# Two key tiles' scores in one run over three PSUM slots, and a planner with other durations and ranks

## The chip, the cores and the metric

The kernel runs on one core of one Trainium2 chip. The metric is the device time of one execution in microseconds. PE is TensorE, DVE is VectorE, ACT is ScalarE, POOL is GpSimd, SP is SyncE; L414 is line 414 of the kernel.

## The reference

A thresholded attention is followed by a feed-forward block with a quick GELU. All numbers are float32.

```python
# q, k, v: (8, 8, 576, 64)   tau = 0.02
scores = scale * np.matmul(q, k.transpose(0, 1, 3, 2))
thresh = np.max(scores, axis=-1, keepdims=True) - tau
scores = np.where(scores >= thresh, scores, -1000000000.0)
scores = scores - np.max(scores, axis=-1, keepdims=True)
attn = np.exp(scores)
attn = attn / (np.sum(attn, axis=-1, keepdims=True) + 1e-09)
attn_out = np.matmul(attn, v)
x = attn_out.transpose(0, 2, 1, 3).reshape(4608, 512)
h = x @ w_in                                  # w_in  (512, 2048)
g = h * (1.0 / (1.0 + np.exp(-1.702 * h)))
out = g @ w_out                               # w_out (2048, 512)
```

The two weights come as 64-bit floats and are turned into 32-bit ones on the chip.

## The kernel before

**Attention.** The 64 heads are 32 pairs (`n`), four pairs a batch. A pair's two heads lie on partitions 0 to 63 and 64 to 127. The scores are held transposed, keys on partitions: four tiles of 128 keys with both heads side by side (128 x 1152), and a tail tile with the last 64 keys of both heads (128 x 576). For a pair, in turn:

- `load_qk`, `load_v` (SP's DMA queue), `prep` (L390, DVE transposes q and k), `prep_kd` (L395, POOL copies the tail keys of both heads into a block-diagonal `kd`).
- `scores` (L414, two matmuls at a time on half of PE's rows; the tail, L407, with `kd` on the full array) into PSUM slots of the pool `psA`, which has three slots of two banks. Each slot is copied to SBUF by `keep` (L437, ACT) and then is free.
- `in_groups` (L451, DVE: transpose and reduce over groups of 32 keys), `over_tiles` (L457, L462), `over_groups` (the folds, L471, L472) give the maximum; `lower` and `spread_max`, or for the first pairs `lower_rows`, `row_out` and `row_in` (a round trip by DMA), spread the threshold; `sub` (L523 to L528, DVE), `mask` (L534, ACT), `exps` (L538, ACT).
- `values` (L552, half of PE's columns, 40 records a pair) into a `psA` slot that stays taken until `place_x`; sums of the weights by PE (`sums_by_pe`) for pairs 0 to 4, by DVE afterwards (`one_group`, L595); `spread_sums` (L604, L606); `place_x` (L623, DVE) scales the values, writes them into `xT` and frees the slot.

**Feed-forward.** 18 blocks of 256 tokens. The first two run plainly: `mm1_0` (L678) for 16 column tiles `j`, `tanh` (ACT) and `gelu_0` (DVE), then `mm2` (L660). The next twelve run `mm1` (L638), `tanh`, `gelu` (L650), and `second` (L825): a product in seven half-size products P1 to P7 in place of eight, for which POOL makes sums of weight quarters once (`t_sum`, L785) and sums of activations for each block (`s_sums`, L791 to L793; `s_last`, L804). The last four blocks run in two pairs by `two_blocks`, where the first product is made in the same way (`product1`, L743) from sums made by `w_sum` (L717, DVE and POOL) and `x_sum` (L726, DVE), which need all of the attention's buffers to be free. `read` (L840, L847) takes the products out of PSUM.

**Order.** The kernel orders its work itself. Each piece is a task with an engine, a cost in us, a rank, the tasks it comes after, and the pools it takes from and gives to. `run_in_order` plays the tasks through on the host: whenever an engine is free it starts the ready task of lowest rank whose pools have room. The order in which tasks start is the order of the instructions in each engine's queue; on the chip an instruction waits only for the data and buffers it needs, and for its queue.

```python
def task(engine, cost, rank, f, *a, after=(), take=(), give=(), lag=0.06):
    if 0 <= rank < LAST:
        rank += CV.get(f.__name__, 0.0) + (EARLY if a[0] < 2 * NPAIR else LATER).get(f.__name__, 0.0)
...
for rank, i in sorted(queue):
    take = tasks[i][6]
    if all(free[pool] >= take.count(pool) for pool in set(take)):
        break
```

`EARLY` and `LATER` are the ranks' corrections for pairs 0 to 7 and the rest. The conversion of a weight piece is `cv_ex` (L353), `cv_frac` (L367, L371) and `cv_end` (L379) on DVE and `cv_power` on ACT; 32 pieces of 128 x 512 come by POOL's DMA queue.

Of the kernel before, what the change touches and what calls it, by code (L numbers as in the profile page):

```python
# [10 lines left out]
FP32 = mybir.dt.float32  # L11
# [19 lines left out]
def kernel(  # L31
# [97 lines left out]
    for x in ("raw0", "raw1", "qkT0", "qkT1", "mb"):  # L129
# [6 lines left out]
        "lower_rows": -1.89,  # L136
        "values": 1.63,
        "exps": 1.38,
        "load_qk": -1.72,
        "prep": -1.69,  # L140
        "load_v": 1.46,
        "mask": 1.64,
        "over_groups": -1.9,
        "sub": -1.05,
        "one_group": 0.95,
        "scores": 0.67,
        "spread_sums": 1.4,
        "sums_by_pe": 2.29,
        "in_groups": 0.61,
        "keep": -1.15,  # L150
    }
    LATER = {
        "in_groups": 0.38,
        "mask": -0.74,
    }
    CV = {
        "cv_power": 0.15,
        "cv_frac": 0.13,
    }

    def task(engine, cost, rank, f, *a, after=(), take=(), give=(), lag=0.06):
        if 0 <= rank < LAST:
            rank += CV.get(f.__name__, 0.0) + (EARLY if a[0] < 2 * NPAIR else LATER).get(f.__name__, 0.0)
        tasks.append((engine, cost, rank, f, a, [x for x in after if x is not None],
                      take, give, lag))
        return len(tasks) - 1
# [3 lines left out]
    def run_in_order():  # L170
# [10 lines left out]
        started = 0  # L181
        while events:
# [18 lines left out]
            for engine, queue in ready.items():  # L201
# [12 lines left out]
                heapq.heappush(events, (now + tasks[i][1], 0, i))  # L214
# [187 lines left out]
    def scores(n, t, c):  # L402
        qT, kT = mats[n, 0], mats[n, 1]
        ps = psA.tile([P, 2, 512], FP32, name="ps", tag="ps")
        if t == NKT:
            for i in range(2):
                nc.tensor.matmul(  # L407
                    ps[:, i, 0:SH], lhsT=kd, rhs=qT[:, ts(i, SH)],
                    start=True, stop=True,
                )  # L410
            del mats[n, 0], mats[n, 1]
        else:
            for h in range(2):
                nc.tensor.matmul(  # L414
                    ps[:, h, 0:SH],
                    lhsT=kT[ts(h, D), ts(t, P)], rhs=qT[ts(h, D), ts(c, SH)],
                    start=True, stop=True,
                )
        pss[n, t, c] = ps

    def scores_of(n, t, cs):
        for c in cs:
            scores(n, t, c)
# [474 lines left out]
    FFU = 1.722  # L898
# [3 lines left out]
    for i in range(len(pieces)):  # L902
# [9 lines left out]
        a = task("POOL", 2.4, rank, load_w, i, after=w_loads[-1:], take=place, lag=5.0)  # L912
        w_loads.append(a)
        e = task("DVE", 0.43, rank, cv_ex, i, after=[a])
        m = task("ACT", 0.79, rank, cv_power, i, after=[e])
        a = task("DVE", 1.14, rank, cv_frac, i, after=[e])

        over = [ready_w[y] for y in range(i) if i >= n_in and stage(y) == (i - n_in) // PER_STAGE]
        ready_w.append(task("DVE", 0.7, rank, cv_end, i, after=[a, m] + over, give=place))
# [8 lines left out]
    def first_blocks():  # L928
        xs = list(placed.values())[-NPAIR:]
        for j in range(NFC):  # L930
# [7 lines left out]
            a = task("ACT", 0.6, FIRST, tanh, j, after=ffn[-1:], take=("io",))  # L938
            gelus[j] = task("DVE", 0.69, FIRST, gelu_0, j, after=[a], give=("psM", "io"))
        for i in range(PLAIN * BLK // P):  # L940
# [7 lines left out]
            a = task("ACT", 0.6, FIRST, half, i, after=ffn[-1:], take=("osb",), give=("psM",))  # L948
            task("SP", 0.6, FIRST, store_0, i, after=[a], give=("osb",), lag=2.2)

        for x in range(4):
            for k in range(2):
                after = t_ready[-1:] + (ffn[-1:] if x > 1 else ffn[2 * NFC : 2 * NFC + 1])
                t_ready.append(
                    task("POOL", 3.0, FIRST, t_sum, x, k, after=after + ready_w[n_in:])
                )

    def feed_forward(blk):
# [3 lines left out]
        for j in range(HF):  # L962
            for f in range(2):
# [6 lines left out]
            a = task("ACT", 0.6, FIRST, tanh, j, after=ffn[-1:], take=("io",))  # L970
            gelus[j] = task(
                "DVE", 0.69, FIRST, gelu, j, after=[a, last_mm2.get(j // 4)],
                give=("psM", "io"),
            )
            if j % 2:
                sums.append(task("POOL", 2.5, FIRST, s_sums, j // 2, after=[gelus[j - 1], gelus[j]]))
        second(blk, 0, {j: [gelus[j]] for j in range(HF)}, sums)

    def second(blk, w, ready, sums):
# [4 lines left out]
        for x, p in order:  # L984
            js = ((0, 4), (4, 8), (4, 7), (7, 8))[p]
            after = ffn[-1:] + t_ready
# [15 lines left out]
            if x == P6:  # L1002
                lasts = [task("POOL", 1.6, FIRST, s_last, k, w, after=ffn[-1:]) for k in range(2)]
            if x == P1:
                a = task("ACT", 0.35, FIRST, read, blk, x, after=ffn[-1:], take=("osb", "osb"))
            else:
                a = task(
                    "DVE", 0.84 if x == P5 else 0.42, FIRST, read, blk, x, after=ffn[-1:] + reads,
# [8 lines left out]
    def two_blocks(blk):  # L1017
# [4 lines left out]
        for x in range(4):  # L1022
            if first:
                done_w.append([task("DVE", 0.66, LAST - 1.0, w_sum, x, 0, nc.vector, after=done_w[-1:][0] if done_w else xs)])
            after = (xd[-1:] or xs) + (done_w[x][:1] if first else []) + last_product1
            xd.append(task("DVE", 0.66, LAST - 1.0, x_sum, blk, x, after=after))
        if first:
            for k in range(1, HF // 2):
                for x in range(4):
                    after = xs + done_w[x - 1][-1:] + done_w[x][-1:]  # L1030
                    done_w[x].append(
                        task("POOL", 1.5, FIRST, w_sum, x, k, nc.gpsimd, after=after)
# [3 lines left out]
        for j in range(HF):  # L1036
            reads = [None] * 7
            for x in range(7):
# [6 lines left out]
                if x == P3:  # L1045
                    after += xs
# [5 lines left out]
                if x == P1:  # L1052
                    a = task("ACT", 0.35, FIRST, read1, j, x, after=ffn[-1:], take=("hs",), give=bank)
                else:
                    a = task(
                        "DVE", 0.84 if x == P5 else 0.42, FIRST, read1, j, x,
# [3 lines left out]
            for h in range(2):  # L1060
                a = task("ACT", 0.6, FIRST, tanh1, j, h, after=[reads[P5 if h == 0 else P3]], take=("io",))
                g1[j, h] = task(
                    "DVE", 0.8, FIRST, gelu1, j, h, after=[a, last_mm2.get(j // 4), g1.get((j, 0))],
                    give=("io", "hs") if h else ("io",),
                )
            if j % 2:
                sums.append(task(
                    "POOL", 2.5, FIRST, s_sums, j // 2, after=[g1[j - 1, 0], g1[j, 0]]
# [5 lines left out]
        a = task("DVE", 1.3, FIRST, s_sum1, 0, after=again + ffn[-3:-2])  # L1074
        b = task("DVE", 1.3, FIRST, s_sum1, 1, after=[a] + ffn[-1:])
        c = task("DVE", 1.3, FIRST, s_sum1, 2, after=[b])
# [7 lines left out]
    for n in range(NP):  # L1084
# [4 lines left out]
        slow = 1.2 if n < NPAIR else 1.0  # L1089
# [11 lines left out]
        pq = task("DVE", 0.77, r, prep, n, 0, after=[lq], take=own(n, "qkT0"), give=own(n, "raw0"))  # L1101
        pk = task("DVE", 0.77, r, prep, n, 1, after=[lk], take=own(n, "qkT1"), give=own(n, "raw1"))
        pd = task("POOL", 0.5, r, prep_kd, n, after=[pk], take=("kd",))
# [5 lines left out]
        mx = []  # L1109
        for t in range(NKT + 1):  # L1110
            tail = t == NKT
            copies = []
            if tail or n >= WHOLE:


                cs = range(1 if tail else 2)
                a = task(
                    "PE", (1.2 if tail else 1.35) * slow, r, scores_of, n, t, cs, after=[pq, pk] + ([pd] if tail else []) + after,
                    take=("psA", "s_t") if tail else ("psA", "psA") + own(n, "s_m"),
                    give=own(n, "qkT0", "qkT1") + ("kd",) if tail else (),  # L1120
                )
                after = [a]
                copies = [task("ACT", 0.65, r, keep, n, t, c, after=[a], give=("psA",)) for c in cs]
            else:
                for c in range(2):

                    a = task(
                        "PE", 0.6 * slow, r, scores, n, t, c, after=[pq, pk] + after,
# [3 lines left out]
                    copies.append(task("ACT", 0.65, r, keep, n, t, c, after=[a], give=("psA",)))  # L1132
            mx.append(task("DVE", 0.76 if tail else 1.37, r, in_groups, n, t, ALU.max, after=copies))
# [100 lines left out]
```

## Time and profile before

| | us |
|---|---|
| timed runs | 1387.58, 1389.71, 1392.3 |
| profiled execution, span | 1385.8 |
| PE busy | 1330.6 |
| DVE busy | 1123.9 |
| ACT busy | 639.6 |
| POOL busy | 299.8 |

Busy times say how much an engine did, not whether it set the end; that is read stage by stage, from the waits and from the chain of work that ended last. A matmul's end is modelled in the profile, so differences between starts are used below. The profiler shows two records for each float32 matmul.

### The profile page before, as it was taken

Reading aid. Unit: us, or ns where it says so; the run is one execution under the profiler, and the core shown is the slowest. Engines: PE = TensorE matmul, PEld = TensorE weight load, DVE = VectorE, ACT = ScalarE, POOL = GpSimd, SP = SyncE. Lnnn points to the kernel's source line nnn. Section 1 sums busy time; section 2 is a strip of 40 time slices with the busy share of each in tenths; the row PEclk is TensorE's granted clock in tenths of the full one; section 3 lists DMA queues with packets and bytes.
Section 4 is the critical chain, followed back from the end, with each engine's and each line's share of the span. In section 5 each row is a group of like instructions: output and inputs, shape, how many; then the busy total and the mean of one; then the engine's idle time right before and its main releaser. Section 6 shows DMA issues by size and latency. Waiting matters only on the chain.

```text
span 1385.8 us, 18139 instructions
## 1 busy us (share of the span) xinstructions
PE 1330.6 (96%) x6792; PEld 1004.2 (72%) x6792; DVE 1123.9 (81%) x1906; ACT 639.6 (46%) x822; POOL 299.8 (22%) x362
## 2 busy tenths in 40 slices
PE   5778999999999999999999999999999999799999
PEld 3446864477777777777777777777777777688887
DVE  7989999978888888889888888888888888762642
ACT  5864663555454545454545445444545454120210
POOL 1121222212131213122212212121212224321120
PEclk9889999999999999999999999999999999999999
DMA  8674973211111111111111011111111100000000
GB/s 173 200 235 132 301 256 67 68 22 22 41 27 41 27 41 21 39 26 34 26 33 35 18 42 26 42 26 42 26 34 25 42 1 8 9 1 16 16 1 31
DMA packets 205379, 78.70 MB, mean 57 GB/s; under 512 B 192747, under 2 KB 192747, under 8 KB 205291
## 3 DMA queue, kind: packets, MB, share of 16 engines
q1 hardware_dynamic: 195723, 43.71, 15.0%
q0 software_dynamic: 7200, 33.55, 7.0%
q8 instruction: 53, 0.87, 0.2%
q10 hardware_dynamic: 2368, 0.30, 0.2%
q14 instruction: 35, 0.29, 0.1%
HBM read 68.05 MB, written 9.47 MB: 56 GB/s over the span
## 4 chain that ended last, share of the span: by engine, by line
PE 84%; DVE 12%; DMA 1%; issue 1%; SPq 1%; ACT 0%; DVEq 0%
PE hps L638 25%; PE ops L825 24%; PE ps L414 9%; PE pv L552 9%; PE ps L743 4%; PE hps L678 4%; PE ps L825 3%; PE ops L743 3%; DVE part L451 3%; PE ps L407 2%; DVE arena L523 2%; SPq L278 1%; PE den L552 1%; DVE red L472 1%; DVE arena L390 1%
## 5 line engine op out<-in xcount | busy, mean ns | idle before, releaser
L451 DVE TRANSPOSE_TENSOR_REDUCE part<-arena 128x36 f32<-128x1152 f32 x236 | 315.3, 1354 | 71.6 <-ACT arena L437 70.9
L638 PE MATMUL hps<-xT,w_in 128*128 128x256 f32 x1536 | 346.3, 382 | 0.0
L638 PEld LDWEIGHTS hps<-xT,w_in 128*128 128x128 f32 x1536 | 287.9, 190 | 56.3 <-issue 18.5
L437 ACT COPY arena<-ps 128x576 f32<-128x576 f32 x288 | 171.1, 641 | 292.3 <-PE ps L414 271.2
L825 PE MATMUL ops<-w_out,arena 128*128 128x256 f32 x896 | 205.5, 382 | 0.0
L534 ACT ACTIVATE arena<-arena 128x1152 f32<-128x1152 f32 (+1 forms) x160 | 168.2, 1060 | 76.3 <-DVE arena L523 70.2
L538 ACT ACTIVATE arena<-arena,shift,scl 128x1152 f32<-128x1152 f32 (+1 forms) x160 | 194.4, 1243 | 1.9
L825 PEld LDWEIGHTS ops<-w_out,arena 128*128 128x128 f32 x896 | 168.0, 190 | 32.8 <-issue 10.0
L523 DVE TENSOR_TENSOR arena<-arena 128x1152 f32<-128x1152 f32 x128 | 190.6, 1528 | 1.3 <-DMA arena<-row 0.6
L414 PE MATMUL ps<-arena 64*128 64x288 f32 x1024 | 162.0, 439 | 21.9 <-DVE arena L390 11.0
L791 POOL TENSOR_TENSOR arena<-arena 128x256 f32<-128x256 f32 x56 | 46.5, 831 | 566.5 <-DVE arena L650 467.4
L414 PEld LDWEIGHTS ps<-arena 64*128 64x128 f32 x1024 | 90.7, 191 | 84.7 <-issue 52.0
L825 PE MATMUL ops<-arena 128*128 128x256 f32 x672 | 149.9, 379 | 0.3 <-DVE osb L847 0.3
L825 PEld LDWEIGHTS ops<-arena 128*128 128x128 f32 x672 | 127.6, 190 | 18.0 <-DVE osb L847 0.7
L552 PE MATMUL pv<-arena 128*64 128x288 f32 x960 | 126.0, 414 | 1.2 <-issue 1.2
L647 ACT ACTIVATE th<-hps 128x512 f32<-128x512 f32 x112 | 66.4, 593 | 127.0 <-PE hps L638 106.0
L552 PEld LDWEIGHTS pv<-arena 128*64 128x64 f32 x960 | 67.0, 138 | 55.7 <-issue 14.6
L390 DVE STREAM_TRANSPOSE arena<-arena 128x576 f32<-128x576 f32 x64 | 48.3, 762 | 37.7 <-PE ps L407 35.3
L804 POOL TENSOR_TENSOR arena<-arena 128x512 f32<-128x512 f32 x28 | 57.5, 2060 | 98.6 <-PE ops L825 98.5
L650 DVE SCALAR_TENSOR_TENSOR arena<-th,hps 128x512 f32<-128x512 f32 x96 | 63.8, 665 | 8.8 <-ACT th L647 8.8
L395 POOL COPY kd<-arena 64x64 f32<-64x64 f32 x64 | 17.6, 275 | 235.0 <-DVE arena L390 191.2
L847 DVE SCALAR_TENSOR_TENSOR osb<-ops,osb 128x256 f32<-128x256 f32 x98 | 38.6, 405 | 34.9 <-PE ops L825 33.2
(122 smaller groups left out, 1422.4 us busy)
## 6 DMA issues: line engine op xcount, KB each, us to landing
arena<-in_q_dram SPq DMA_DIRECT2D x128, 72.0 KB, 2.2
out_dram<-osb SPq DMA_DIRECT2D x36, 256.0 KB, 2.0
arena<-in_k_dram SPq DMA_DIRECT2D x124, 72.0 KB, 2.2
arena<-in_v_dram SPq DMA_DIRECT2D x64, 128.0 KB, 2.4
w_out<-in_moe_w_in_dram POOLq DMA_DIRECT2D x12, 512.0 KB, 5.8
arena<-in_moe_w_out_dram POOLq DMA_DIRECT2D x12, 512.0 KB, 5.4
w_out<-in_moe_w_in_dram POOLq DMA_DIRECT2D x12, 511.6 KB, 7.0
arena<-in_moe_w_out_dram POOLq DMA_DIRECT2D x12, 511.6 KB, 6.3
```

Source lines behind the costliest of these rows:

```text
L414: nc.tensor.matmul(ps[:, h, 0:SH], lhsT=kT[ts(h, D), ts(t, P)], rhs=qT[ts(h, D), ts(c, SH)], start=True, stop=True,)
L437: nc.scalar.copy(out=o, in_=pss.pop((n, t, c))[:, :, 0:SH])
L451: nc.vector.tensor_reduce(out=o, in_=i, axis=AXL.X, op=op, apply_transpose=True)
L523: nc.vector.tensor_tensor(out=s, in0=s, in1=mb, op=ALU.subtract)
L534: nc.scalar.activation(out=s, in_=s, func=AF.Prelu, alpha=STEEP)
L538: nc.scalar.activation(out=s, in_=s, func=AF.Exp, scale=scl, bias=shift)
L552: nc.tensor.matmul(o[c][ts(h, D), 0:SH], lhsT=lhsT, rhs=rhs, start=(t == 0), stop=(t == NKT),)
L638: nc.tensor.matmul(hidden[j][:, ts(f, BLK)], lhsT=w_in[:, c, ds((f * HF + j) * P, P)], rhs=xTs[blk][:, c, :], start=(c == 0), stop=(c == N ...
L647: nc.scalar.activation(out=ths[j], in_=hidden[j], func=AF.Tanh, scale=GELU_SCALE / 2)
L650: nc.vector.scalar_tensor_tensor(out=g[:, :, j, :], in0=two(ths.pop(j)), scalar=1.0, in1=two(hidden.pop(j)), op0=ALU.add, op1=ALU.mult,)
L743: nc.tensor.matmul(places[j, x], lhsT=left[:, c, ts(j, P)], rhs=right[:, c, :], start=(c == 0), stop=(c == 1),)
L825: nc.tensor.matmul(banks[blk][k][:, ts(o, HM)], lhsT=left[:, j, :], rhs=right[:, j, :], start=(j == 0), stop=(j == HF - 1),)
```

## The change

Pairs from the seventh on (`WHOLE = 6`) make their scores by `scores_two`: two key tiles in one run of eight matmuls, in three `psA` slots taken together. The first 320 queries of each tile have a slot of their own, the last 256 queries of both tiles share the third. `keep_two` copies them, four copies for two tiles as before (128 x 640 and 128 x 512 in place of 128 x 576). The eight `t_sum` tasks come after the first product of block 2 instead of after the first blocks' first product, and only the products that read them come after them in the plan. The first `two_blocks` comes after all pairs in the plan. `tau_terms` comes after the first `prep`. The planner has new costs, a delay between engines (`LAG`), a cost for a change of PE's layout (`ENTER`), and new ranks for nearly every task.

```diff
     EARLY = {
-        "lower_rows": -1.89,
-        "values": 1.63,
...
+        "exps": 18.84,
+        "in_groups": 6.03,
...
+    LAG = {"PE": 0.26, "DVE": 0.18, "ACT": 0.22, "POOL": 0.18}
...
+    ENTER = (0.2, 0.1, 0.1)
...
+                if engine == "PE":
+                    last, mode = mode, MODES[tasks[i][3].__name__]
+                    cost += ENTER[mode] if mode != last else 0.0
...
+    FAR = S - BLK
+
+    def scores_two(n, t):
+        near = [psA.tile([P, 2, 512], FP32, name="ps", tag="ps") for _ in range(2)]
+        far = psA.tile([P, 2, 512], FP32, name="ps", tag="ps")
+        for u, part in ((0, 0), (0, 1), (1, 1), (1, 0)):
+            qs = ds(FAR, BLK) if part else ds(0, FAR)
+            for h in range(2):
+                o = far[:, h, ts(u, BLK)] if part else near[u][:, h, 0:FAR]
                 nc.tensor.matmul(
-                    ps[:, i, 0:SH], lhsT=kd, rhs=qT[:, ts(i, SH)],
+                    o, lhsT=mats[n, 1][ts(h, D), ts(t + u, P)], rhs=mats[n, 0][ts(h, D), qs],
                     start=True, stop=True,
                 )
...
+    def keep_two(n, t, c):
+        if c == 0:
+            sT[n, t] = seat_scores(n, t).rearrange("p (h s) -> p h s", h=2)
+        o = sT[n, t][:, :, ds(FAR, BLK)] if c else sT[n, t][:, :, 0:FAR]
+        nc.scalar.copy(out=o, in_=pss.pop((n, t, c)))
...
-        for x in range(4):
-            for k in range(2):
-                after = t_ready[-1:] + (ffn[-1:] if x > 1 else ffn[2 * NFC : 2 * NFC + 1])
-                t_ready.append(
-                    task("POOL", 3.0, FIRST, t_sum, x, k, after=after + ready_w[n_in:])
-                )
...
+            if j == T_AFTER and blk == PLAIN:
+                for y in range(8):
+                    after = t_ready[-1:] + ffn[-1:] + ready_w[n_in:]
+                    t_ready.append(task("POOL", 2.4, FIRST, t_sum, *divmod(y, 2), after=after))
...
-            after = ffn[-1:] + t_ready
+            after = ffn[-1:]
+            if x in T_OF:
+                after += t_ready[: T_OF[x]]
...
-                if x == P3:
+                if x == P3 or first:
                     after += xs
...
+        if n == 0:
+            tasks[tau_done][5].extend([pq, pk])
...
+            if n >= WHOLE and not tail:
+                if t % 2 == 0:
+                    a = task(
+                        "PE", 1.94, r, scores_two, n, t, after=[pq, pk] + after,
+                        take=("psA",) * 3 + ("s_m",) * 2,
+                    )
+                    after = [a]
+                b = task("ACT", 0.6, r, keep_two, n, t, 0, after=[a], give=("psA",))
+                c = task(
+                    "ACT", 0.48, r, keep_two, n, t, 1, after=[a, b] + far, give=("psA",) * (t % 2)
+                )
+                far = [c] if t % 2 == 0 else []
+                copies = [b, c]
...
-            mx.append(task("DVE", 0.76 if tail else 1.37, r, in_groups, n, t, ALU.max, after=copies))
+            mx.append(task("DVE", 0.66 if tail else 1.27, r, in_groups, n, t, ALU.max, after=copies))
```

## The prediction

> **What bounds the kernel now.** I read the page's busy table and slices first, then the windows by stage, the waits of TensorE, and the timeline where those waits lie.
>
> ```profile
> PE 1330.6 (96%) x6792; PEld 1004.2 (72%) x6792; DVE 1123.9 (81%) x1906; ACT 639.6 (46%) x822; POOL 299.8 (22%) x362
> ...
> PE   5778999999999999999999999999999999799999
> DVE  7989999978888888889888888888888888762642
> ```
>
> PE is full from about slice 5 on; only the start (DVE as full) and one slice near the end are not. So three stages: a start set by DVE, a long even stretch set by PE, and a passage to the last four blocks. The windows confirm it: PE is busy 150.00 of 150.00 us in each window from 350 to 1100, DVE 128. Who PE waits for:
>
> ```profile
> PE den L552 <- ACT arena L538: 16.8, 5, 5.6
> ...
> PE ps L414 <- DVE xT L623: 9.3, 4, 6.5
> PE ps L743 <- DVE arena L726: 7.5, 2, 6.3
> ```
>
> The first is in the first 122 us, before any feed-forward. The other two are places where work on PE is lost later: scores waiting for a place_x to give a PSUM slot back, and a product waiting for the sums of the last blocks.
>
> The even stretch, from PE's timeline:
>
> ```profile
> 502.77 1.24 PE L414 MATMUL ps<-arena 64*128 64x288 f32 x8
> 503.94 1.99 PE L825 MATMUL ops<-w_out,arena 128*128 128x256 f32 x8
> 505.87 1.24 PE L414 MATMUL ps<-arena 64*128 64x288 f32 x8
> ...
> 512.06 1.24 PE L414 MATMUL ps<-arena 64*128 64x288 f32 x8
> 513.23 1.24 PE L407 MATMUL ps<-arena,kd 128*128 128x288 f32 x4
> 514.30 20.88 PE L638 MATMUL hps<-xT,w_in 128*128 128x256 f32 x96
> 535.12 1.24 PE L414 MATMUL ps<-arena 64*128 64x288 f32 x8
> ```
>
> Take differences of starts. A record is one of the two passes of a matmul. 96 records of 256 columns take 20.82 us, so about 0.215 each after one change of layout is taken off, 0.84 ns a column. Eight records of the short run L825 should take 1.72 and take 1.93; eight of the scores, two at a time on half the rows, should take 0.97 and take 1.17. So each change of layout costs 0.20 to 0.21 us. The tail tile (L407, full array) costs 1.08 to 1.10 after scores; in the five places where it stands between two full-array runs it takes 0.97, and the run ahead of it ends 0.09 earlier.
>
> **What the Trainium skill says.** "TensorEngine Tiling (Array Packing)", Key Properties: changing the tiling mode drains the engine. The trace agrees, at 0.2 us a change. "SBUF — State Buffer", two separate sides: VectorE and GpSimd share a port pair as an exclusive lock, held for a whole instruction. The trace shows it plainly (DVE's timeline, then POOL's):
>
> ```profile
> 268.06 0.18 DVE L471 COPY fold<-red 64x36 f32<-64x36 f32 x1
> 268.27 2.23 DVE L472 TENSOR_TENSOR red<-red,fold 64x36 f32<-64x36 f32 x1
> 270.54 2.26 DVE L471 COPY fold<-red 32x36 f32<-32x36 f32 x1
> 272.83 2.27 DVE L472 TENSOR_TENSOR red<-red,fold 32x36 f32<-32x36 f32 x1
> ```
> ```profile
> 268.07 4.69 POOL L785 TENSOR_TENSOR arena<-w_out,arena 128x1024 f32<-128x1024 f32 x2
> 272.72 4.63 POOL L785 TENSOR_TENSOR w_out<-w_out 128x1024 f32<-128x1024 f32 x2
> ```
>
> An operation of 0.2 us lasts as long as t_sum's 2.35 us. Transposes and group reductions beside t_sum at 214 to 218 kept their 0.74 and 1.3 us. "TensorE: Matmul & The Clock Gate", What's actually happening: after an idle window of some 3.4 us the array runs at half clock. The trace agrees: after the 6.45 us idle the next scores take 2.29 instead of 1.24.
>
> **Part 1, the scores in one run (even stretch).** The built program's order on PE repeats every two pairs, before and after. Before: values 2 runs, scores 8 runs of 4 matmuls, tail 2, full-array runs 8. After: values 2, scores 4 runs of 8, tail 2, full-array 8, and each tail now stands between full-array runs. Columns are the same (320+256 for 288+288), so are matmuls. Saved: four ends of scores runs, 4 x 0.21 = 0.84; two tails 2 x 0.105 = 0.21; two full-array runs ahead of a tail 2 x 0.09 = 0.18. Together 1.23 of a period of 74.69 us (the values of two periods start at 463.59 and 538.28 in the chain of waits). From 351 us, where the tenth pair begins, to the last pair are 11 periods: 11 x 1.23 = 13.5 us; I take 13, bounds 0 and 14.
>
> What could cost something here. The shapes 64x320 and 64x256: a weight load lasts 191 ns and the shortest matmul record would be 213, so it stays hidden; two loads one behind the other would not, but then the present runs, 240 ns a record, could not take 1.17 either. Zero, at most 0.1 a run. ACT: four copies per two tiles as before; exps of 1152 and 576 columns take 1349 and 866 ns in the first 250 us, so 64 columns more or less are 54 ns, up on one copy and down on the next: zero. ACT is idle half the time. The wait that is added: a run takes all three psA slots. Within a pair, 8 full-array matmuls (3.6 us) stand after the first run, and the four copies, 4 x 0.64 = 2.6, begin during it: hidden. Between pairs, 16 matmuls (6.9 us) stand between the second pair's values and the next scores; place_x must end in them. Today it ends 1.6 us after the values (values to 1140.72, place_x to 1142.3). Hidden, with 5 us to spare. Behind a late place_x would queue everything on PE. DVE's busy 128 of 150 becomes 130 of 150: no new bound. SP issues the same DMAs; a load of v that waits for the third pair's values now stands ahead of the fourth pair's row, but both are due near 85 us: zero, at most 2.
>
> **Part 2, the passage.** Before, after the last values only 8 feed-forward matmuls are left:
>
> ```profile
> 1174.49 1.14 PE L552 MATMUL pv<-arena,v_t 128*64 128x288 f32 x8
> 1175.56 3.72 PE L825 MATMUL ops<-w_out,arena 128*128 128x256 f32 x16
> ...
> 1187.28 2.04 PE L743 MATMUL ps<-arena 128*128 128x256 f32 x4 [6.28 <-DVE arena L726]
> ```
>
> From 1175.56 to the second products at 1237.37 are 120 matmuls, 51.5 us at 0.43; they take 61.8: 10.3 lost, of which 7.5 idle and the rest half clock. After the change 28 matmuls follow the last values: 12.0 us. DVE's chain (place_x, w_sum, x_sum in turn) took 11.7 before the third product could start; that now lies beside the 12.0, and two products more. Later sums take up to 16.6 us and four output reads stand between them on DVE: I leave 2 us. Saved: 8, bounds 5 and 10. The new dependence of product1 on all pairs holds back nothing, as no pair is left then.
>
> **Part 3, the start.** PE does the same 67.2 us of attention before the first feed-forward. Summing DVE's instructions in both orders with this trace's means puts the fourth place_x at 117.7 before (it ended at 119.9) and 116.1 after; the prepared transposes no longer wait for tau (6.0 us, of which about 1 us gates the first scores). So feed-forward begins 0 to 2 us earlier than 122.4. Conversions are more bunched; the eighth, and the thirteenth and fourteenth, stand only 7 us behind the one that frees their buffer, and a load takes 5.8 to 7.0: up to 2 us back. Net zero.
>
> Then t_sum. The planner now places all eight after the first product of block 2, but a queue only keeps order; what an instruction waits for is its data (before, they began at 207.5 though placed later). In POOL's new order all eight stand behind the ninth pair's kd copy. I follow DVE from the sixth place_x, which is 5 us earlier as no t_sum stands beside the last conversions: kd near 240, four t_sum at 240 to 250, the other four from about 254, when the last product of the first blocks has read its data. They fall on the folds of the eighth pair and on its subtractions: about 9 and up to 9 us lost on the way to the seventh place_x, where it was 8 on the eighth. PE reaches the ninth pair's scores near 259 and would wait until 264 to 275. By PE's order this stands against today's 262. If the lock costs as little as elsewhere, the whole start gains 8 (waits of 9.2 us gone); if all of it falls on the path, it loses 5. I take 0, between the ends, as no row shows which.
>
> **Sum.** 0 - 13 - 8 = -21 on the span of 1385.8, so 1365. The timed runs are 1387.58, 1389.71 and 1392.3, so the profiled execution lies 3.9 below their median; I keep that distance: 1369.
>
> **Rivals.** (a) The forecast, chance 0.52: 1369. (b) The sums' lock misses the path at the start and everything else holds, 0.23: -8 more, 1361. For it speaks that DVE's order has group reductions between, which the lock spares. (c) Runs join but PE waits a little for three slots, 0.5 to 1 us a period, so the 13 shrink to 3 and the start loses 5: 1369 + 10 + 5 = 1384, of which about half is no difference that counts; 0.18. Against it, the 5 us of slack. (d) Slower, 0.07: place_x of the second pair comes late in every period, because DVE, in order and nine tenths full, has subtractions or reductions of the other pair ahead of it, and scores that need all three slots wait. It decides from 6.9 us after the values; each us beyond costs 11. Paying back the 21 takes 2 us a period; with 3 us, 33 - 21 = +12: 1402. Against it, today 1.6 us. The change doing nothing is excluded by the built order: 113 scores runs become 67.
>
> A measurement of this kernel can tell about 0.3%, 4.2 us, from no change: below 1385.5 is faster, above 1393.9 slower. From (a), (b) and two thirds of (c): 0.87 faster; the rest of (c), 0.06, the same; (d) 0.07. The range takes (a), (b) and most of (c): 1356 to 1384, the lower end by the best bounds (-8 -14 -10 = -32, less likely together).
>
> **What would show it.** Even stretch: values two periods apart 73.5 us instead of 74.69, scores runs of 16 records near 2.13, tails 0.97, no PE idle. Passage: no idle above 2 us before the first products of L743's successor. Start: t_sum at 240 to 270 with DVE folds of 2.3 beside it. It is wrong if the waits list shows scores waiting for place_x all along, or if scores runs last over 2.3 us.

## The result, and the profile after

The changed kernel takes 1394.93 us (median of 4 runs, 1392.64 to 1398.04), the kernel before, run beside it, 1390.41 us (1387.58 to 1392.3). The ratio is 1.0043, 95% interval 1.0022 to 1.0064: slower by some 0.4%. The forecast was 1369 us with a range of 1356 to 1384.

The page of the changed kernel, busy times and slices (its profiled span is 1393.5 us):

```profile
PE 1320.7 (95%) x6792; PEld 1008.7 (72%) x6792; DVE 1131.6 (81%) x1906; ACT 644.6 (46%) x822; POOL 321.3 (23%) x362
...
PE   5867998979999999999999999999999999999999
DVE  6987988979797989889797979797979899762642
```

PE's busy time has fallen by 9.9 us, and the slice with a 7 near the end is gone, but slices 3, 4, 7 and 9 have become worse. DVE's row shows the new rhythm of two pairs, 9 and 7 in turn. TensorE's waits (us in total, times, longest):

```profile
PE den L627 <- ACT arena L613: 24.8, 8, 10.3
PE ops L900 <- DVE osb L922: 11.9, 10, 5.1
...
PE ps L487 <- DVE xT L698: 7.4, 1, 7.4
PE ps L462 <- DVE arena L447: 6.5, 1, 6.5
```

The lines of before have moved: L552 is L627, L538 L613, L623 L698, L847 L922, L825 L900, L414 is L462 for pairs 0 to 5 and L487 for the joined runs. The wait of the last blocks for their sums (7.5 us before) is gone. New are products that wait for `read` (L922; 0.3 us in all before), in the even stretch and in the passage. The waits for exponentials (L613) have grown from 16.8 us, and scores now wait for a transpose (L447) as late as 111 us; before, such waits lay in the first 20 us.

To place the difference, sum the columns of TensorE's records at 0.833 ns each, half of that for scores and values (64 rows or 64 columns wide). The sum, 1246.0 us, is the same for all kernels here, so the time at which each reaches the same sum can be compared:

| TensorE's work done, us | before | changed | difference |
|---|---|---|---|
| 67.2 (feed-forward begins) | 122.2 | 127.0 | +4.8 |
| 130 | 187.1 | 197.7 | +10.6 |
| 220 | 293.7 | 309.3 | +15.6 |
| 1040 | 1163.2 | 1174.3 | +11.1 |
| 1060 | 1194.1 | 1201.8 | +7.7 |
| 1245 | 1381.3 | 1388.9 | +7.6 |

So the opening loses 15.6 us, the even stretch gives 4.5 and the passage 3.4. The forecast had 0, 13 and 8.

In most of the runs below the planner is replaced by a written list of its tasks, so that one part of an order can be changed with the rest held. With the planner's own list this is the same program:

```diff
-    run_in_order()
+    [tasks[i][3](*tasks[i][4]) for i in PLAN]
```

| run | median, us | ratio to the kernel before, 95% interval |
|---|---|---|
| changed kernel | 1394.9 | 1.0043 (1.0022 to 1.0064) |
| e3, `read` of P2 one place ahead | 1385.4 | 0.9972 (0.9960 to 0.9984) |
| e7, e3 with the joined runs cut in two | 1402.7 | 1.0107 (1.0082 to 1.0132) |
| e4, weight sums behind the last `place_x` | 1389.8 | 0.9993 (0.9977 to 1.0008) |
| e1, old order to pair 6's scores | 1381.3 | 0.9945 (0.9927 to 0.9963) |
| e10, old order to pair 5's scores | 1385.2 | 0.9975 (0.9962 to 0.9988) |
| e11, old order to pair 3's scores | 1395.9 | 1.0044 (1.0031 to 1.0058) |
| e2, old order on SP's queue alone | 1397.3 | 1.0051 (1.0033 to 1.0070) |
| e6, conversions 3 to 5 later | 1399.3 | 1.0073 (1.0052 to 1.0094) |
| e13, conversions 1 to 5 earlier | 1389.9 | 1.0002 (0.9991 to 1.0012) |
| e8, a weight load at its old cost | 1373.7 | 0.9893 (0.9873 to 0.9913) |
| e5, e1 + e3 + e4 | 1367.2 | 0.9846 (0.9826 to 0.9865) |
| e9, e5 with `t_sum` behind pair 6's `place_x` | 1364.1 | 0.9821 (0.9806 to 0.9837) |
| e12, the same behind pair 7's | 1364.7 | 0.9816 (0.9803 to 0.9830) |

### The profile page after: what moved, and what is told of

It is laid out like the page before. It is cut to its first block, busy times and chain, and to the rows that moved or that the text cites. A ratio compares the mean times of both kernels' runs of the same rounds, so it can differ in the third digit from the quotient of the medians.

```text
span 1393.5 us, 18070 instructions
## 1 busy us (share of the span) xinstructions
PE 1320.7 (95%) x6792; PEld 1008.7 (72%) x6792; DVE 1131.6 (81%) x1906; ACT 644.6 (46%) x822; POOL 321.3 (23%) x362
## 4 chain that ended last, share of the span: by engine, by line
PE 50%; DVE 34%; ACT 5%; DMA 4%; SPq 4%; issue 2%; DVEq 0%; POOL 0%; ACTq 0%
PE ops L900 18%; DVE part L526 9%; PE hps L713 8%; DVE arena L598 7%; PE pv L627 6%; PE ps L487 5%; PE ps L818 4%; SPq L335 4%; PE ps L900 3%; DVE arena L725 3%; PE ops L818 3%; ACT arena L613 2%; DVE arena L447 2%; DVE arena L603 2%; DVE arena L572 2%
## 5 line engine op out<-in xcount | busy, mean ns | idle before, releaser
L713 PE MATMUL hps<-xT,w_in 128*128 128x256 f32 x1536 | 342.2, 381 | 0.0
L498 ACT COPY arena<-ps 128x640 f32<-128x640 f32 x208 | 123.4, 643 | 209.7 <-PE ps L487 209.7
L900 PE MATMUL ops<-w_out,arena 128*128 128x256 f32 x896 | 208.2, 384 | 6.8 <-DVE osb L922 6.8
L613 ACT ACTIVATE arena<-arena,shift,scl 128x1152 f32<-128x1152 f32 (+1 forms) x160 | 200.5, 1253 | 4.2
L900 PEld LDWEIGHTS ops<-w_out,arena 128*128 128x128 f32 x896 | 166.8, 190 | 45.8 <-DVE osb L922 10.4
L598 DVE TENSOR_TENSOR arena<-arena 128x1152 f32<-128x1152 f32 x128 | 181.4, 1445 | 4.6 <-DMA arena<-row 4.6
L900 PE MATMUL ops<-arena 128*128 128x256 f32 x672 | 154.6, 384 | 5.1 <-DVE osb L922 5.1
L900 PEld LDWEIGHTS ops<-arena 128*128 128x128 f32 x672 | 127.8, 192 | 27.9 <-DVE osb L922 5.5
L452 POOL COPY kd<-arena 64x64 f32<-64x64 f32 x64 | 25.0, 390 | 500.0 <-DVE thr L552 330.9
L866 POOL TENSOR_TENSOR arena<-arena 128x256 f32<-128x256 f32 x56 | 60.1, 1073 | 331.3 <-DVE arena L725 225.2
L627 PE MATMUL pv<-arena 128*64 128x288 f32 x960 | 124.8, 411 | 0.0
L487 PE MATMUL ps<-arena 64*128 64x320 f32 (+1 forms) x832 | 115.9, 417 | 7.4 <-DVE xT L698 7.4
L627 PEld LDWEIGHTS pv<-arena 128*64 128x64 f32 x960 | 66.8, 137 | 53.6 <-issue 10.5
L487 PEld LDWEIGHTS ps<-arena 64*128 64x128 f32 x832 | 76.2, 187 | 39.2 <-issue 26.4
L922 DVE SCALAR_TENSOR_TENSOR osb<-ops,osb 128x256 f32<-128x256 f32 x98 | 39.7, 417 | 61.3 <-PE ops L900 59.6
L867 POOL TENSOR_TENSOR arena<-arena 128x256 f32<-128x256 f32 x56 | 69.4, 1240 | 4.4
L447 DVE STREAM_TRANSPOSE arena<-arena 128x576 f32<-128x576 f32 x64 | 48.8, 768 | 23.0 <-DMA arena<-in_q_dram 19.8
```

The costliest lines, as they stand in the source:

```text
L447: nc.vector.transpose(out=dst, in_=raws.pop((n, which)))
L487: nc.tensor.matmul(o, lhsT=mats[n, 1][ts(h, D), ts(t + u, P)], rhs=mats[n, 0][ts(h, D), qs], start=True, stop=True,)
L498: nc.scalar.copy(out=o, in_=pss.pop((n, t, c)))
L598: nc.vector.tensor_tensor(out=s, in0=s, in1=mb, op=ALU.subtract)
L613: nc.scalar.activation(out=s, in_=s, func=AF.Exp, scale=scl, bias=shift)
L627: nc.tensor.matmul(o[c][ts(h, D), 0:SH], lhsT=lhsT, rhs=rhs, start=(t == 0), stop=(t == NKT),)
```

## The even stretch: e3 and e7

The theory after the result: the joined runs save what was forecast, and a wait that was not foreseen takes most of it back. One period of the changed kernel, 74.51 us (values at 410.93 and 485.44), on PE, then DVE, then POOL:

```profile
497.45 3.62 PE L900 MATMUL ops<-arena 128*128 128x256 f32 x16
501.82 1.99 PE L900 MATMUL ops<-w_out,arena 128*128 128x256 f32 x8 [0.75 <-DVE osb L922]
```
```profile
498.82 2.49 DVE L603 TENSOR_TENSOR arena<-arena 64x576 f32<-64x576 f32 x2
501.34 0.43 DVE L922 SCALAR_TENSOR_TENSOR osb<-ops,osb 128x256 f32<-128x256 f32 x1
```
```profile
499.42 1.27 POOL L879 TENSOR_TENSOR arena<-arena 128x512 f32<-128x512 f32 x1 [6.67 <-PE ops L900]
```

The first PE line is P6, the second P7. P7 goes into the other half of P2's bank and waits until `read` has taken P2 out, at 501.34. P2 itself was done when P6 began, at 497.45. `read` stands in DVE's queue behind the two subtractions of the pair's tail (L603), and these take 2.49 us beside GpSimd's `s_last` (L879), where without it they take about 1.5. From P6's start to P7's are 4.37 us instead of 3.46.

The stretched one is the second subtraction, and the margin is small. At 721.93 us `s_last` starts 9 ns ahead of it, and it takes 1.88 us. At 648.45 us `s_last` starts 3 ns ahead; the subtraction keeps its 0.76 us, `s_last` takes 1.90, P7 does not wait, and the period is 73.49 us. So nine of the ten whole periods of this execution have the wait. In all eight profiles that keep this order (the changed kernel, e1, e2, e4, e6, e10, e11, e13) the subtraction is stretched where `s_last` leads by 6 ns or more, and in none where it leads by 5 ns or less.

e3 moves the one instruction, in blocks 3 to 13 (the list of VectorE's tasks):

```diff
 sub(13, 3)
+read(block 4, P2)
 sub(13, 4)
-read(block 4, P2)
```

> One VectorE instruction moved: in the blocks 3 to 13 the reading of product P2 goes one place ahead, before the last two subtractions of the pair's tail instead of behind them. Theory B (joined runs save what was forecast, and the late reading gives it back): the wait of 0.75 us ahead of P7 goes, the period falls from 74.51 to 73.4 to 73.8, eleven periods: 1382 to 1387 us. Rival B2 (VectorE is so nearly full around it that the same delay comes back at the next product or at the placing of x): the period stays above 74.2, 1391 us or more.

Measured: 1385.4. The wait is gone from the list but for one of 5.6 us in the passage, and the values are now at 407.75 and 481.24: a period of 73.49 us. In the same place, DVE:

```profile
494.53 0.40 DVE L922 SCALAR_TENSOR_TENSOR osb<-ops,osb 128x256 f32<-128x256 f32 x1
494.86 2.49 DVE L603 TENSOR_TENSOR arena<-arena 64x576 f32<-64x576 f32 x2
```

The subtractions still take 2.49 us beside GpSimd, but nobody waits for them. Theory B holds; that VectorE is too full (B2) does not. The price of one wait can be read across the runs below that leave `read` where it was, since they meet it in a different number of periods: TensorE's work from 220 to 1040 us takes 861.9 us with six waits (e10), 865.0 with nine (the changed kernel), 866.0 with ten (e1) and 855.8 with none (e3), which is 1.02 us for each.

e7 asks whether it is the joining that saves: e3 with each joined run from pair 8 on cut between its two tiles, and the next group of feed-forward matmuls put there.

```diff
-        for u, part in ((0, 0), (0, 1), (1, 1), (1, 0)):
+        for u, part in (((0, 0), (0, 1)), ((1, 1), (1, 0)))[half]:
```

> As the kernel with the reading of P2 moved (1385.4), but from pair 8 on each joined run of scores is cut in two by the next group of feed-forward matmuls, which goes between its two key tiles: the same matmuls, shapes and slots, four more changes of layout in each period. If the joined runs are what saves the time in the even stretch: four times 0.31 us in each of some eleven periods come back, 1396 to 1401 us. Rival (the layout changes cost nothing there, and the gain comes from the new order's places for values and tails): within 3 us of 1385.

Measured: 1402.7, 17.3 more than e3. The period is 75.08 us (408.14 to 483.22), 1.59 more for four cuts, each of which adds two changes of layout: 0.20 us a change. On PE:

```profile
512.54 1.24 PE L487 MATMUL ps<-arena 64*128 64x320 f32 x8
513.71 1.99 PE L900 MATMUL ops<-arena 128*128 128x256 f32 x8
515.64 1.24 PE L487 MATMUL ps<-arena 64*128 64x256 f32 x8
```

From run to run are 3.10 us, where a joined run of 16 records and the same 8 of L900 behind it take 3.97 for twice the scores (515.85 to 519.82 in the changed kernel). Counted in the traces, a period has 18 changes of layout before, 12 in e3 and 20 in e7, and lasts 74.69, 73.49 and 75.08 us: 0.20 us for each change in both directions. The expectation, 0.31 for a cut, was too low: it was the forecast's 1.23 a period divided by four, but the change takes away six changes of layout, and four cuts add eight.

## The passage: e4

In the changed kernel the weight sums on GpSimd (L792) run from 1172.03 to 1187.3, as soon as their data is there. The plan had them behind the last pair; the queue does not know that. Beside them, DVE, and PE's wait:

```profile
1182.35 1.20 DVE L547 TENSOR_TENSOR red<-red,fold 32x36 f32<-32x36 f32 x1
1183.58 3.76 DVE L670 TENSOR_SCALAR r<-red 32x18 f32<-32x18 f32 x4
1187.37 0.43 DVE L922 SCALAR_TENSOR_TENSOR osb<-ops,osb 128x256 f32<-128x256 f32 x1
```
```profile
1187.85 5.40 PE L900 MATMUL ops<-arena 128*128 128x256 f32 x16 [5.10 <-DVE osb L922]
```

e4 puts one GpSimd copy of one element ahead of the sums; it reads what the last `place_x` writes, so the queue waits there.

```diff
+            def gate():
+                last = xTs[NBLK - 1][0:1, NDC - 1, BLK - 1 : BLK]
+                nc.gpsimd.tensor_copy(out=rebias[0:1, :], in_=last)
+            task("POOL", 0.1, FIRST, gate, after=xs)
```

> One GpSimd copy of a single element is added ahead of the twelve weight sums on GpSimd; it reads the last element that the last pair's placing writes, so that the weight sums can't run beside the last pair's sums on VectorE. Theory C (the weight sums' hold on the shared port stretches the last pair's folds, and so the reading of P2 comes late): the wait of 5.1 us at P7 falls to under 1.5, 1389 to 1392 us. Rival C2 (the twelve sums, begun later, collide with the readings of the first seven products or come too late for the third group of products): new waits of 3 us or more there, 1394 us or more.

Measured: 1389.8, within what was expected. The 12 runs spread from 1382.1 to 1393.0, and the profiled one is the second longest; what spreads them isn't settled. (The expectation names the wrong products: what waits is P5, for the reading of P7, which shares its bank.) DVE now:

```profile
1179.15 0.18 DVE L547 TENSOR_TENSOR red<-red,fold 32x36 f32<-32x36 f32 x1
1179.37 0.71 DVE L670 TENSOR_SCALAR r<-red 32x18 f32<-32x18 f32 x4
```

The fold takes 0.18 instead of 1.20, the next line 0.71 instead of 3.76, and the wait of 5.10 is gone. The sums now run beside VectorE's own sums of the last blocks, which take up to 1.78 us where they had taken 0.69; that costs two waits of 1.15 and 1.05 at the first products. From 1040 to 1060 us of TensorE's work are 23.2 us, where the changed kernel takes 27.5 and the kernel before 30.9. So the passage gives 7.7, near the forecast's 8, once the sums are held back.

## The opening: e1, e10, e11, e2, e6, e13, e8

e1 takes every engine's order from the kernel before up to pair 6's first scores, and from the changed kernel after that.

> Every engine's instructions up to pair 6's first scores in the order of the kernel before; after that the order of the changed kernel, with its costs, scores and ranks untouched. Theory A (the opening is lost to the new order of the first six pairs and of the weights' conversions): the 10.6 us by which TensorE is behind when it has done 130 us of its work (187.1 before, 197.7 after) come back, and some of the 5 after it: 1379 to 1385 us, TensorE at 130 us of work by 187 to 189. Rival A2 (the opening is lost to what both orders now share: tau's terms behind the first transposes, pairs 6 and 7 in joined runs, the table's differences on GpSimd): 1391 to 1396 us.

Measured: 1381.3. TensorE reaches 130 us of its work at 187.5 and 220 at 295.6. The loss is made by the order of this stretch, not by tau's place or the joined runs of pairs 6 and 7.

e10 and e11 take less of the old order.

> The order of the kernel before up to pair 5's first scores only (some 110 us), the changed kernel's from there on. If the opening is lost among the first five pairs and the conversions beside them: TensorE is at 130 us of work by 187 to 190 us and the time is 1380 to 1386 us, as with the longer stretch of the old order. If half of it is lost later, beside the first feed-forward block, where TensorE waits for conversions and gelu (8.8 us in five waits between 136 and 229 us): 1386 to 1391 us.

> The order of the kernel before up to pair 3's first scores (some 60 us), the changed kernel's from there on, with conversions 2 to 5 again ahead of pair 3's subtractions. If the interleaving of pairs 1 and 2 makes the loss (the wait of 10.3 us at 36 us): 1382 to 1387 us. If it is made where pair 3's exponentials and pair 5's q come late (98.5 and 111 us): 1391 to 1397 us.

Measured: e10 1385.2, with feed-forward beginning at 121.0; e11 1395.9, with feed-forward at 129.3, no better than the changed kernel. So about 10 of the 14 us that e1 brings back are lost between pair 3's first scores and pair 5's, some 60 to 110 us, and 4 later.

What happens there in the changed kernel, SP's queue, POOL's and DVE's:

```profile
90.10 11.16 SPq L335 DMA_DIRECT2D arena<-in_q_dram  x4
```
```profile
95.17 0.54 POOL L399 DMA_DIRECT2D arena<-in_moe_w_in_dram  x1 [0.73 <-issue]
```
```profile
108.78 0.78 DVE L447 STREAM_TRANSPOSE arena<-arena 128x576 f32<-128x576 f32 x1 [8.41 <-DMA arena<-in_q_dram]
```

The line of POOL is the last of four weight pieces of 1 MB that are begun within 6 us (from 89.46), and the four issues of pair 5's q take 11.16 us instead of about 2.2. From 90 to 106 us the transfer engines are full (a share of 1.02 of their time, 327 GB/s). e2 gives SP's queue alone the old order.

> Only SP's queue in the opening is in the order of the kernel before (pair 3's lookup rows ahead of pair 4's values, and so on); every other engine as in the changed kernel. If the queue's own order is what makes VectorE wait for q and rows (19.8 us after, 1.8 before): 1383 to 1389 us. If it is the bunched loads of the weights that fill the transfer engines, whatever the queue's order: 1391 to 1397 us, and pair 5's q still comes 5 us or more late.

Measured: 1397.3; the issues of q take 11.43 us. The forecast's "zero, at most 2" for the queue's order holds.

e6 moves what starts the four loads: each needs a buffer that the end of an earlier conversion gives back.

```diff
-cv_frac(3) cv_end(3) cv_frac(4) cv_end(4) cv_frac(5) cv_end(5)
 sub(3, 0) ... sub(3, 4) prep(5, 0) prep(5, 1)
+cv_frac(3) cv_end(3) cv_frac(4) cv_end(4) cv_frac(5) cv_end(5)
```

> The changed kernel with one group moved on VectorE: the last steps of the weight conversions 3, 4 and 5 (nine instructions) go behind pair 5's transposes instead of ahead of pair 3's subtractions, so that their buffers, and with them four loads of 1 MB, come free some 10 us later than pair 5's q is issued. Theory A1 (these loads, begun within 6 us, fill the transfer engines and delay q): VectorE's wait of 8.4 us for pair 5's q falls under 3, TensorE at 85 us of work comes at 142 to 145 instead of 149, and the time is 1387 to 1391 us. Rival A3 (the wait for q only stands in for others: pair 4's exponentials, the weights themselves): TensorE is still at 147 or later there, 1393 to 1397 us.

Measured: 1399.3, a miss. The issues of q take 3.94 us and the wait for q 2.18, as A1 said; but the pieces behind came later too. VectorE then waits for them (3.72 us for one), ScalarE's part of those conversions stands in its queue ahead of a copy of scores, and scores wait 11.8 us for that copy. So the loads do delay q, but moving them on did not pay. The question is when their traffic can be carried. The starts of the loads of pieces 6 to 12, counted from 0:

| | us |
|---|---|
| before | 65.8, 71.7, 73.6, 75.9, 82.8, 86.2, 94.3 |
| changed | 54.6, 82.4, 89.5, 91.6, 93.4, 95.2, 114.7 |
| e10 | 65.1, 71.5, 73.4, 75.6, 81.8, 85.2, 93.2 |
| e11 | 66.0, 83.0, 92.2, 94.3, 96.1, 97.9, 117.3 |
| e6 | 56.2, 83.9, 91.0, 106.5, 108.3, 110.0, 120.6 |

The three that lose start piece 7 only at 82 to 84 us, where the others have four of these started by 76. Windows show what was carried (length of the window, busy us of PE, PEld, DVE, ACT and POOL, then clock, share of the transfer engines, GB/s). In the kernel before:

```profile
60.00:90.00 30.00, 25.70 (x154) 13.11 (x152) 28.22 (x55) 20.87 (x27) 7.43 (x14) 0.83 0.72 224
90.00:120.00 30.00, 18.57 (x122) 9.41 (x120) 26.12 (x50) 22.38 (x28) 5.10 (x10) 0.94 0.80 221
```

In the changed kernel, where the first 30 us carry only 151 GB/s:

```profile
60.00:90.00 30.00, 26.00 (x180) 13.50 (x176) 28.44 (x54) 25.75 (x34) 2.08 (x6) 1.00 0.53 151
90.00:120.00 30.00, 14.19 (x72) 6.79 (x74) 20.34 (x32) 14.70 (x18) 7.50 (x15) 0.72 0.78 225
```

In the old order the ends of conversions 1 to 3 stand ahead of pair 3's group maxima; in the new one all of 1 to 5 stand behind them. e13 moves only these ten tasks back to there.

> The changed kernel with the last steps of the weight conversions 1 to 5 moved ahead on VectorE, to where the kernel before has them: three behind pair 4's transposes, two between pair 3's group maxima (after them, all five stand behind those maxima, four of them ahead of pair 3's subtractions). Nothing else moves. Theory A4 (their late place leaves the load buffers full, so that no weight piece is loaded from 55 to 82 us, and then four at once, when pair 5's q is due): loads at 72 to 86 us, the wait for q under 3 us instead of 8.4, 1383 to 1389 us. Rival A5 (the order of the pairs' own work makes the loss, the conversions only fill the time): pair 3's maxima end 7 us later, and with them its exponentials; 1392 us or more.

Measured: 1389.9 over 12 runs (1385.3 to 1391.1). The loads start at 72.8, 74.6, 76.2, 81.9 and 85.6, the issues of q take 2.20 us, the share of the transfer engines from 90 to 106 us is 0.49, VectorE does not wait for q at all, and feed-forward begins at 120.9. The profiled execution, one of the two fastest, has 1383.2 and reaches 220 us of work at 299.2, like e10. So the place of the conversions makes the loss between 60 and 110 us, since nothing else moved: 10 us by the profiles, 5 by the medians; the median is 0.9 above the expected range. In return pair 3's row comes late: TensorE waits once for 15.1 us at 100. Why most runs are up to 6 us longer than the profiled one isn't settled; the wait for `read`, which the profiled one has eight times, could account for at most 2.

What is left, 4 us between e10 and e1, lies for the most part in waits for gelu and for conversions between 136 and 229 us. The changed kernel has five (2.0, 1.6, 1.4, 1.9 and 1.9), e10 three (1.8, 1.3 and 2.5), e1 three short ones (0.7, 0.6 and 1.1). No run takes them away alone.

e8 changes one number of the planner.

```diff
-        a = task("POOL", 1.1, rank, load_w, i, after=w_loads[-1:], take=place, lag=5.0)
+        a = task("POOL", 2.4, rank, load_w, i, after=w_loads[-1:], take=place, lag=5.0)
```

> One number of the planner: a load of a weight piece costs 2.4 us again, as before, instead of the 1.1 that its two issues take on GpSimd. If the new cost (the issue's time, not that of the 1 MB it moves) is what bunches the conversions and the loads: 1382 to 1389 us. If the ranks do it whatever this cost: 1391 to 1398 us.

Measured: 1373.7, more than expected, and not for the reason given. The bunch is still there (loads at 90.4, 92.5, 94.3 and 96.1, VectorE waiting 8.38 us for q), and feed-forward begins at 128.4, no earlier than in the changed kernel. The order differs later: 220 us of work is reached at 297.0, the periods are 73.49 (472.67 to 546.16) to 73.68 without a wait for `read`, and the passage takes 22.3. One cost moved the whole plan to an order in which the second and third of the three faults happen not to occur. It shows how much of this result is the draw of an order; it doesn't show that the load's cost makes the bunch.

## Together, and the table differences: e5, e9, e12

> The three edits that each took time off the changed kernel, together: the order of the kernel before up to pair 6's first scores, the reading of P2 one place ahead, and the GpSimd copy ahead of the weight sums. If the three losses are separate, their gains against 1394.9 add up (13.6, 9.5 and 5.1): 1364 to 1371 us. If one of them hides another (the opening's order shifts the period, so that the reading is late in another place, or the passage starts from another point): 1372 to 1379 us.

Measured: 1367.2. The three gains add up. By stage, against the kernel before: the opening to 220 us of work 0.0, from there to 1040 -13.6, the passage -7.5. Against both kernels it is faster.

Its largest later wait is 9.2 us at 270, for pair 6's `place_x`, beside `t_sum`. e9 adds a second gate, ahead of `t_sum`.

```diff
+                def t_gate():
+                    last = xTs[2 * S // BLK][0:1, 6 % NPAIR, HT - 1 : HT]
+                    nc.gpsimd.tensor_copy(out=rebias[0:1, :], in_=last)
```

> As the kernel with the three edits together (1367.2), with one more GpSimd copy of a single element ahead of the eight differences of the output weights: it reads the last element that the placing of pair 6's x writes. In the kernel with the three edits these differences run from 242.8 to 266.7 us, VectorE's instructions beside them take some 10 us longer than alone, and TensorE waits 9.2 us for that placing. Theory D (the shared port is that wait): the placing comes at 258 to 262 us instead of 270, the wait falls under 2.5, 1357 to 1361 us. Rival D2 (the scores that wait need pair 6's values anyway, or the differences run into pair 8's sums instead): 1364 us or more.

Measured: 1364.1. The placing comes at 257.3 instead of 269.6 and its wait is gone, but the next placing, pair 7's, now costs one. That is 3 us where 6 to 10 were expected; D is right about the wait, and its rival about where it goes. e12 gates behind pair 7 (`7 % NPAIR`).

> As the run with the differences of the output weights behind the placing of pair 6's x (1364.1), but behind that of pair 7's. There pair 6's placing came at 257.3 us instead of 269.6, and the next one, pair 7's, then ran beside the differences and held TensorE for 5.8 us at 280. Theory D: with neither placing beside the differences that wait falls under 1.5, 1358 to 1361 us. Rival D3 (TensorE there waits for pair 7's chain on VectorE whatever GpSimd does, or the differences, done only by about 290 us, hold up the sums of the gelu halves behind them): 1363 us or more.

Measured: 1364.7, no gain over e9: D3. The wait of e9, and that of e12:

```profile
280.47 1.44 PE L487 MATMUL ps<-arena 64*128 64x320 f32 x4 [5.79 <-DVE xT L698]
```
```profile
293.43 4.21 PE L487 MATMUL ps<-arena 64*128 64x320 f32 x16 [5.83 <-DVE arena L447]
```

The wait moves with the differences, now to pair 9's transpose, which stands on DVE behind folds of 1.6 to 2.3 us. GpSimd needs 18.6 us for them, and at each of the three places tried short VectorE operations fall into this time that TensorE ends up waiting for. These are three cases; where a gate pays is read from them and not tested further.

## Why the prediction was wrong

The sum "0 - 13 - 8 = -21" is, to a microsecond, what e5 shows (0.0, -13.6, -7.5). For the even stretch and the passage that bears out the savings; the 0 for the opening is no hit, as e5 has the old order there. The changed kernel has three faults of order that the forecast did not see.

**The start, "Net zero": the step that failed most, +15.6.** The forecast put the fourth `place_x` at 116.1 by summing VectorE's instructions. It ended at 128.6. The sum had no waits for transfers in it, and after the first transposes VectorE waits for them some 14 us in that time: 8.41 for pair 5's q, 3.36 for a row, the rest for k and a weight piece. In the kernel before these waits are 2.9 us, and the same sum fell 2.2 short there too (117.7 for 119.9). "Conversions are more bunched ... up to 2 us back" priced the bunch by what the conversions wait for, each load at its old 5.8 to 7.0 us. In the changed kernel the loads of the first weight take 8.0 to 11.3 in the median (5.8 to 7.3 before), and what stands behind it is another queue's q; besides, ahead of the bunch the transfer engines stood half idle. The bounds, -8 to +5, came from `t_sum` alone. `t_sum` began at 257.9, not near 240, since it stands behind the ninth pair's `kd` copy, itself late; its wait, 7.4 us, replaced one of 6.5. That part was near nothing, as forecast.

**The even stretch, -13: it gave 4.5; the saving was right, "no new bound" was not.** The forecast's period was 74.69 - 1.23 = 73.46; e3 has 73.49. The wait for three slots is indeed hidden: in the even stretch no scores wait for `place_x`. The failed step is "DVE's busy 128 of 150 becomes 130 of 150: no new bound". The 130 was right (64.7 in 74.5), but it asked only whether VectorE is full. A product waits for one short `read` in VectorE's queue, and the new order puts `s_last` beside what is ahead of it. That is 1.02 us in nine of ten periods. The forecast looked for new waits at the slots, not at each bank's reading.

**The passage, -8: it gave 3.4.** The failed step is "DVE's chain ... now lies beside the 12.0". The 12.0 us of products were counted as work that waits for nothing, but P5 among them needs VectorE's reading of P7, and that stands in VectorE's queue behind the last pair's folds. Before, the weight sums stretched one of these four folds (1.17 us, at 1174.02); now they stretch all four (1.14 to 1.21 us). The forecast knew the rule, "a queue only keeps order; what an instruction waits for is its data", used it for `t_sum`, and not for `w_sum`.

**The rivals.** (d), slower by late slots, did not happen: its mechanism is absent. (c) had a wait of "0.5 to 1 us a period" and a loss at the start; the size is right, the resource wrong (a bank's reading, not the slots), and the start lost 15, not 5. (b) did not happen.

The Trainium skill fits: "SBUF — State Buffer", Who interferes with whom, says that copies can contend with GpSimd, that operations of two SBUF inputs do, and that `tensor_reduce` never does on trn2; here a fold (two inputs) went from 0.18 to 1.20 us, while a `TENSOR_REDUCE` (L532) beside the same weight sums took 0.36 us, as it did without them. "PSUM — Partial Sum Buffer", PSUM bank collisions raise a hardware error, asks to guard by bank, also for other columns of it; the trace has the wait that follows, P7 in P2's other half held for 0.75 us. No run here shows a collision.

## What to carry to other kernels

A sum of an engine's instructions bounds a stage from below only; before pricing a reorder at zero, go through each queue for what now stands behind what, transfers included, and ask which short instruction another engine waits for. A plan's "after" is no wait on the chip: work on GpSimd that must not run beside VectorE's short operations has to read something that they write, and one copy of a single element (0.2 to 0.6 us) did it here. If an edit comes with a new order, measure the edit under an order held fixed, for the order alone moved this kernel by more than the edit.

## What the runs showed of the hardware

The same four issues on SP's queue took 2.2 us where no such bunch stood beside them, and 11.2 to 11.4 us beside four 1 MB loads begun within 6 us. A change of TensorE's layout cost 0.20 us, whether changes were taken out (six a period) or put in (eight). Where a VectorE subtraction and a GpSimd addition met, which of them was held up hung on some nanoseconds: with the addition 6 ns or more ahead the subtraction took 1.74 to 1.88 us, otherwise 0.76. Weight sums on GpSimd beside VectorE's sums of the same size slowed both: 1.75 us on GpSimd where it takes 1.28 alone, 1.78 on VectorE where it takes 0.69.
